# Attention and expert mixture on one core: loading the second batch's q and k behind all weights, in two-token runs, and turning them on TensorE

## The chip, the cores and the metric

The kernel runs on one core of one Trainium2 chip. The metric is the time of one execution on the device, in microseconds (us). Profiles are of one execution each; their time axis starts at the first instruction.

Engines: TensorE (PE; its weight loads are PEld), VectorE (DVE), ScalarE (ACT), GpSimd (POOL), SyncE (SP). DMAs of the loads that convert float32 to bf16 are issued from GpSimd, the plain stores and the DMA transposes from SyncE. Lines such as L679 are lines of the kernel's file; the changed kernel has other line numbers for the same statements, and both are named where it matters.

## The reference

Streaming attention with four sink tokens and a window of 128, then a dense mixture of four experts whose outputs are weighted by normalised probabilities:

```python
# q, k, v: (4 batches, 8 heads, 768 tokens, 64); all float32
scores = q @ k.T / 8, kept where key < 4 or 0 <= query - key < 128   # else -1e9
x = softmax(scores) @ v                      # (4, 768, 8 * 64) -> x: (3072, 512)
p = domain_probs / domain_probs.sum(-1)      # (3072, 4)
out = sum over e of p[:, e] * (relu(x @ w1[e]) @ w2[e])   # w1[e]: 512 x 1024, w2[e]: 1024 x 512
```

## The kernel before

The kernel is written as a list scheduler in Python: while it is being built it keeps a clock for each engine and for the DMA (the *issue clock*), and always emits next what should be ready first. The chip does not see this clock. What the clock decides is **the order of the instructions on each engine and in each DMA queue**, and an engine executes its instructions in that order. A wrong clock costs time only where it puts an instruction that is not ready in front of one that is.

Batch 0 goes through a plain mixture (a first layer, L679, and a second layer, L828). Batches 1 to 3 go through a seven-product form (L775), which needs sums of hidden blocks that VectorE makes (S0, S1, S2 and one in place). While batch b's mixture runs, batch b+1's attention is threaded in between.

How q and k get to have the head dimension on the partitions: batch 0's are loaded in runs of two tokens, regrouped on ScalarE or VectorE and transposed on TensorE. Those of the other batches are loaded token by token and turned by a DMA transpose that SyncE issues:

```python
def load_nat(b, tb):                       # one block of 128 tokens, q and k
    both = sb.tile([P, 2, H, D], BF16, name="qkn", tag="qkn", bufs=NQB)
    for i, src in enumerate((q, k)):
        nc.gpsimd.dma_start(out=both[:, i], in_=src[b, :, tb * P:(tb + 1) * P, :].rearrange("h p d -> p h d"))
    ...
    lands(("qk", b, tb), 3 * H * P * D * 4)

def turn_nat(b, tb):
    nc.sync.dma_start(out=qkT[b][..., tb * P:(tb + 1) * P]..., in_=nat[b, tb]..., transpose=True)
    turned_at[b, tb] = max(t["pe"], landed["qk", b, tb]) + TURN          # TURN = 3500 ns

def lands(key, nbytes):                    # the DMA's issue clock
    dma["at"] += nbytes / 350.0
    landed[key] = dma["at"] + 1500
...
        if not att.more() and not loaded:  # batch 0's attention is done: queue batch 1's loads
            nat_loads(1, range(2)); v_loads(1, 0); gates_by_row()
            nat_loads(1, range(2, NQB)); ...
            loads += [(load_w1, 3), (load_w2, 3)]        # the last expert's weights, last
            turns += [(1, tb) for tb in range(NQB)]
```

The sums, and a buffer that two things share: S2 has the tag `wide2`, and so has the output tile of batch 0's last pair of token blocks, which SyncE stores.

```python
                nc.vector.tensor_add(S[0][:, e], H21, H22)
                nc.vector.tensor_sub(H21, H11, H21)
                nc.vector.tensor_sub(S[1][:, e], S[0][:, e], H11)
...
                S[2] = mo.tile([P, E, QF, P], BF16, name="S2", tag="wide2", bufs=1)
                nc.vector.tensor_sub(S[2][:, e], H12, S[1][:, e])
# batch 0's outputs: out_sb[g] = mo.tile(..., name="osb0", tag=f"wide{g}", bufs=1)
                nc.sync.dma_start(out=out[r:r + P, :], in_=dst)
```

The hidden blocks (`hps`) go through four PSUM banks, which VectorE empties in batches 1 to 3 (L696). When VectorE stands still, TensorE can make four more and then has to stop.

The softmax here doesn't subtract the row's maximum and nothing guards it: scores larger than these inputs give would overflow.

## Time and profile before

| | |
|---|---|
| time, median (range) | 423.35 us (420.43 to 504.98, 3 runs; the 504.98 is a single outlier) |
| span of the profile | 420.6 us |
| TensorE busy | 379.2 us |
| VectorE busy | 257.1 us |
| mean granted TensorE clock | 0.955 |

Three rows of the page, part 2. Each digit is one of 40 equal slices (10.5 us each) in tenths: of the engine's busy share for PE, of the granted clock for PEclk, of the mean busy share of the DMA engines for DMA; 9 means 90% or more.

```profile
PE   5597891499999995999999999999999999999995
...
PEclk9589987599999996999999999999999999999999
DMA  9999999999423899131159911111301111010101
```

TensorE is nearly full from the 17th slice on. Before that it has two dents, the 1 and 4 in the seventh and eighth slices and the 5 in the sixteenth, and the clock's digits drop beside both (5 in the eighth, 6 in the sixteenth). The timeline of TensorE shows the first: start, duration, engine, line, operation, output<-inputs, shapes, count, and in brackets the idle time just before and what ended it.

```profile
78.94 0.51 PE L449 MATMUL sps<-qkT 64*128 64x256 bf16 x4 [13.83 <-DMA qkT<-qkn]
79.37 1.89 PE L679 MATMUL hps<-xT,w 128*128 128x256 bf16 x8
81.05 2.77 PE L828 MATMUL acc<-w,H 128*128 128x512 bf16 x8
```

The scores of batch 1 (L449) stand in front of the rest of batch 0's mixture and wait 13.83 us for the DMA transposes of q and k. The eight first-layer matmuls behind the wait take 1.68 us until the next start, where eight warm ones take 0.87. What else the DMA had to do at that time is in the issue order of GpSimd, whose lines are the loads (L131 q and k, L207 v, L219 and L224 weights):

```profile
55.89 4.42 POOL L207 DMA_DIRECT2D vx<-in_v_dram  x5
60.27 0.79 POOL L219 DMA_DIRECT2D w<-in_moe_w_dram  x1
61.26 0.89 POOL L224 DMA_DIRECT2D w<-in_moe_w_dram  x1 [0.20 <-issue]
```

The five v loads shown, twelve q/k loads ahead of them and one v load more, all in single-token runs, stand in front of the last expert's weights, which are issued at 60 us. The second hole, again from the timeline of TensorE, and beside it that of VectorE:

```profile
162.22 3.57 PE L679 MATMUL hps<-xT,w 128*128 128x256 bf16 x16 [5.11 <-DVE H L696]
165.59 0.54 PE L499 MATMUL od<-vx,aT 128*128 128x65 bf16 x6
```

```profile
161.15 0.42 DVE L741 TENSOR_TENSOR S<-H,S 128x512 bf16<-128x512 bf16 x1 [5.85 <-DMA out_dram<-osb]
161.49 0.68 DVE L696 SCALAR_TENSOR_TENSOR H<-hps,gates 128x512 bf16<-128x512 f32 x1
```

VectorE stands 5.85 us at S2 (L741), on the store whose buffer S2 reuses. The evictions of `hps` (L696) are behind it, and TensorE runs out of banks for 5.11 us. The sixteen matmuls behind the hole take 3.37 us until the next start, instead of 1.75. SyncE's queue at that time, in its order:

```profile
138.79 2.61 SPq L143 DMA_TRANSPOSE qkT<-qkn  x2
...
142.71 7.35 SPq L143 DMA_TRANSPOSE qkT<-qkn  x3
...
150.78 1.40 SPq L143 DMA_TRANSPOSE qkT<-qkn  x1
152.28 2.08 SPq L519 DMA_TRANSPOSE xT<-onat  x1
154.45 1.22 SPq L843 DMA_DIRECT2D out_dram<-osb  x2
```

### The profile page before, as it was taken

To read this page: it belongs to the slowest core of one execution; us is meant where nothing else is said; L and a number is where in the kernel's file an instruction comes from. 1 tells how busy PE (TensorE), PEld (TensorE's weight loads), DVE (VectorE), ACT (ScalarE), POOL (GpSimd) and SP (SyncE) were. 2 spreads that over 40 slices of the span, in tenths; PEclk is the share of its full clock that TensorE was granted. 3 is DMA by queue.
4 is the path that set the end of the run, shared out by engine and by line. 5 is a ranking of instruction groups with operands and counts; after the bars stand their busy time and mean duration, and the time that the engine had idled before them with its cause. 6 is when DMAs were issued, how large, how long until landed. Compare 5 with 4: busy or idle time off the path is not lost.

```text
span 420.6 us, 8232 instructions
## 1 busy us (share of the span) xinstructions
PE 379.2 (90%) x3530; PEld 299.5 (71%) x3530; DVE 257.1 (61%) x551; ACT 99.5 (24%) x161; POOL 70.3 (17%) x109
## 2 busy tenths in 40 slices
PE   5597891499999995999999999999999999999995
PEld 2365461266666663887888888788888888888884
DVE  3535551056645466957967967957749558485570
ACT  3556531154444421023111113221010000100000
POOL 8861281134010353000102000000000000000000
PEclk9589987599999996999999999999999999999999
DMA  9999999999423899131159911111301111010101
GB/s 170 191 194 210 184 155 155 140 115 213 30 26 51 145 194 151 51 37 51 53 51 119 197 25 51 52 27 51 77 0 51 51 51 50 2 51 2 50 2 50
DMA packets 108560, 37.10 MB, mean 88 GB/s; under 512 B 95988, under 2 KB 102228, under 8 KB 108524
## 3 DMA queue, kind: packets, MB, share of 16 engines
q0 software_dynamic: 72832, 17.31, 46.7%
q1 hardware_dynamic: 35692, 19.27, 21.8%
q8 instruction: 27, 0.44, 0.4%
q14 instruction: 9, 0.07, 0.1%
HBM read 40.45 MB, written 6.34 MB: 111 GB/s over the span
## 4 chain that ended last, share of the span: by engine, by line
PE 72%; DVE 11%; DMA 10%; ACT 3%; POOL 1%; issue 1%; DVEq 0%
PE hps L679 30%; PE acc L775 26%; PE acc L828 9%; DVE H L696 5%; DMA qkT<-qkn 4%; DMA qs<-in_k_dram 3%; PE sps L449 3%; PE od L499 2%; ACT aT L460 2%; DMA qkn<-in_q_dram 2%; DMA out_dram<-osb 1%; DVE S L727 1%; DVE S L741 1%; DVE aT L461 1%; DVE H L728 1%; DVE S L729 1%
## 5 line engine op out<-in xcount | busy, mean ns | idle before, releaser
L679 PE MATMUL hps<-xT,w 128*128 128x256 bf16 x1536 | 191.6, 278 | 7.4 <-DVE H L696 7.3
L679 PEld LDWEIGHTS <-w 128*128 128x128 bf16 x1536 | 149.0, 100 | 34.6 <-issue 13.0
L696 DVE SCALAR_TENSOR_TENSOR H<-hps,gates 128x512 bf16<-128x512 f32 x144 | 94.4, 685 | 23.5 <-PE hps L679 22.4
L460 ACT ACTIVATE aT<-sps 128x1024 bf16<-128x1024 f32 (+1 forms) x46 | 44.1, 959 | 84.9 <-PE sps L449 81.6
L775 PEld LDWEIGHTS <-H 128*128 128x128 bf16 x576 | 56.1, 98 | 7.3 <-issue 0.9
L461 DVE TENSOR_TENSOR aT<-aT,mask 128x1024 bf16<-128x1024 bf16 (+1 forms) x46 | 29.9, 649 | 39.7 <-ACT aT L460 39.6
L789 ACT COPY osb<-acc 128x256 f32<-128x256 f32 x36 | 13.4, 373 | 170.4 <-PE acc L775 166.7
L828 PE MATMUL acc<-w,H 128*128 128x512 bf16 x192 | 46.3, 385 | 0.0
L775 PEld LDWEIGHTS <-S 128*128 128x128 bf16 x432 | 41.9, 98 | 5.1 <-issue 0.3
L690 ACT ACTIVATE H<-hps 128x512 bf16<-128x512 f32 x48 | 28.7, 598 | 39.9 <-PE hps L679 39.9
L207 POOL DMA_DIRECT2D vx<-in_v_dram x24 | 21.3, 904 | 84.6 <-PE od L499 80.6
L775 PE MATMUL acc<-wf,H 128*128 128x256 bf16 x288 | 34.4, 273 | 0.5 <-ACT osb L789 0.5
L775 PE MATMUL acc<-w,S 128*128 128x256 bf16 x288 | 34.4, 273 | 0.0
L775 PE MATMUL acc<-w,H 128*128 128x256 bf16 x288 | 34.2, 273 | 0.0
L449 PE MATMUL sps<-qkT 64*128 64x128 bf16 (+1 forms) x256 | 18.6, 245 | 15.7 <-DMA qkT<-qkn 13.8
L828 PEld LDWEIGHTS <-H 128*128 128x128 bf16 x192 | 18.0, 99 | 19.0 <-issue 1.9
L449 PEld LDWEIGHTS <-qkT 64*128 64x128 bf16 x256 | 8.0, 94 | 25.6 <-issue 19.5
L131 POOL DMA_DIRECT2D qkn<-in_q_dram x18 | 15.8, 880 | 61.8 <-DMA qkT<-qkn 52.1
L838 DVE SCALAR_TENSOR_TENSOR osb<-acc,scale_t,osb 128x512 f32<-128x512 f32 x18 | 13.5, 751 | 17.3 <-PE acc L828 17.1
L499 PE MATMUL od<-vx,aT 128*128 128x65 bf16 x352 | 21.1, 198 | 2.9 <-DVE aT L461 2.9
L499 PEld LDWEIGHTS <-aT 128*128 128x128 bf16 x352 | 17.9, 101 | 5.7 <-DVE aT L461 4.0
L511 DVE TENSOR_TENSOR onat<-od,R 128x256 bf16<-128x256 f32 x48 | 20.4, 424 | 1.7
(77 smaller groups left out, 226.8 us busy)
## 6 DMA issues: line engine op xcount, KB each, us to landing
w<-in_moe_w_dram POOLq DMA_DIRECT2D x8, 1024.0 KB, 18.6
out_dram<-osb SPq DMA_DIRECT2D x24, 256.0 KB
gates<-gate_rows SPq DMA_DIRECT2D x9, 512.0 KB
vx<-in_v_dram POOLq DMA_DIRECT2D x24, 128.0 KB, 7.3
qkn<-in_q_dram POOLq DMA_DIRECT2D x18, 128.0 KB, 6.8
qkn<-in_k_dram POOLq DMA_DIRECT2D x18, 128.0 KB, 7.2
qraw<-in_q_dram SPq DMA_DIRECT2D x2, 256.0 KB
kraw<-in_k_dram SPq DMA_DIRECT2D x2, 256.0 KB
```

The costliest lines, as they stand in the source:

```text
L131: nc.gpsimd.dma_start(out=both[:, i], in_=src[b, :, tb * P:(tb + 1) * P, :].rearrange("h p d -> p h d"),)
L207: nc.gpsimd.dma_start(out=vx[tb][:, :, 0:D], in_=v[b, :, tb * P:(tb + 1) * P, :].rearrange("h p d -> p h d"),)
L449: nc.tensor.matmul(sps[ph][:, c:c + nq * P], lhsT=T[pr, 1, hp, kb * P:(kb + 1) * P], rhs=T[pr, 0, hp, qb * P:(qb + nq) * P], start=True, s ...
L460: nc.scalar.activation(out=a, in_=both[:, :, 0:w], func=AF.Exp, scale=scale)
L461: nc.vector.tensor_mul(a, a, m[:, None, :].to_broadcast([P, 2, w]))
L499: nc.tensor.matmul(od[:, qi, ph], lhsT=a[:, ph, c:c + P], rhs=vx[kb][:, 2 * hp + ph, 0:DX], start=(g == 0 and i == 0), stop=(i == len(term ...
L511: nc.vector.tensor_mul(o[:, :, hp].rearrange("p q (h d) -> p q h d", h=2), od[:, :, :, 0:D], R.to_broadcast([P, 2, 2, D]),)
L679: nc.tensor.matmul(h[:, i].rearrange("p (q n) -> p q n", q=2), lhsT=w1_sb[e][:, db, fb * P:(fb + 1) * P], rhs=xT[b, g][:, :, db], start=(i ...
L690: nc.scalar.activation(out=dst, in_=h, func=AF.Relu)
L696: nc.vector.scalar_tensor_tensor(out=dst, in0=h, scalar=0.0, in1=gate, op0=ALU.max, op1=ALU.mult,)
L775: nc.tensor.matmul(x, lhsT=self.operand(b, g, e, m)[:, f], rhs=forms[e][m][:, f], start=(i == 0 and m in ("P1", "P2", "P5")), stop=(i == n ...
L828: nc.tensor.matmul(op, lhsT=H[:, fb // QF, fb % QF, s], rhs=w2_sb[e][:, fb, :], start=(fb == 0), stop=(fb == NFB - 1),)
```

## The change

Its intent: take the first hole away by loading what batch 0's mixture still needs (the last expert's weights) ahead of batch 1, load batch 1's q and k in two-token runs and transpose them on TensorE as for batch 0, count DMA time by rows in the issue clock, and hold S2 back until the store should be done. The core of the diff:

```diff
-    PIECES = {b: [(0, 2), (G, 2), (2 * G, 2)] if b == 0 else [(0, NQB)] for b in range(B)}
+    PIECES = {b: [(0, 2), (G, 2), (2 * G, 2)] for b in range(2)}
...
-    def lands(key, nbytes):
-        dma["at"] += nbytes / 350.0
-        landed[key] = dma["at"] + 1500
+    ROW = {64: 31.0, 128: 40.0, 512: 97.0, 1024: 172.0}
+    def lands(key, rows, cols):
+        dma["at"] += rows * ROW[cols] / 16
+        landed[key] = dma["at"] + 2200
...   (load_qk: batch 1's pieces in tiles of their own, tag "qs", bufs=1)
+                if b == 1:
+                    self.todo += [("regroup", b, g, 0)] + [("transposes", b, g, hp) for hp in range(NHP)]
...
+                self.S_at[u] = t["dve"] + 60          # the other products no longer wait for S2
                 self.waiting.remove(u)
-                if busy((b, g), "P3"):
+                if busy((b, g), "P3") or t["dve"] < self.stored:
                     break
...
-                self.S_at[b, g, e] = dve(QF * P, rate=1.9, fixed=100)
+                self.S4_at[b, g, e] = dve(QF * P, rate=1.9, fixed=100)
...
                 nc.sync.dma_start(out=out[r:r + P, :], in_=dst)
+                self.stored = at + 4500
...
-            nat_loads(1, range(2))
-            v_loads(1, 0)
             gates_by_row()
-            nat_loads(1, range(2, NQB))
-            for g in range(1, NG):
-                v_loads(1, g)
             loads += [(load_w1, 3), (load_w2, 3)]
-            turns += [(1, tb) for tb in range(NQB)]
+            for g in range(NG):
+                loads += [(load_qk, 1, g), (load_v, 1, (2 * g,)), (load_v, 1, (2 * g + 1,))]
```

More of the change, by code (lines that the diff above doesn't have):

```diff
@@ L119, in load_qk @@
             both = mo.tile([P, 2, H, T * D], BF16, name="qs", tag="gates", bufs=2)
-            for i, src in enumerate((q, k)):
-                nc.gpsimd.dma_start(
-                    out=both[:, i], in_=src[b, :, s0:s0 + P * T, :].rearrange("h (p t) d -> p h (t d)", t=T),
-                )
-            nat[b, piece] = both
-            lands(("qk", b, piece), 2 * H * P * T * D * 4)
-            return
+        else:
+            both = sb.tile([P, 2, H, T * D], BF16, name="qs", tag="qs", bufs=1)
+        for i, src in enumerate((q, k)):
+            nc.gpsimd.dma_start(
+                out=both[:, i], in_=src[b, :, s0:s0 + P * T, :].rearrange("h (p t) d -> p h (t d)", t=T),
+            )
+        if b:
+            dma["at"] = max(dma["at"], pool(0, fixed=2400))
+        nat[b, piece] = both
+        lands(("qk", b, piece), 2 * H * P, T * D)
     def load_nat(b, tb):
@@ L136, in load_nat @@
         dma["at"] = max(dma["at"], at)
-        lands(("qk", b, tb), 3 * H * P * D * 4)
+        lands(("qk", b, tb), 2 * H * P, D)
     def turn_nat(b, tb):
@@ L160, in load_first @@
                 nat[0, half, name, "raw"] = x
-            lands(("first", half), 2 * 4 * P * T * D * 4)
+            lands(("first", half), 8 * P * 29 // 40, T * D)
     def copy(engine, out, in_):
@@ L212, in load_v @@
                 dma["at"] = max(dma["at"], pool(0, values_at[b - 1, min(NG - 1, (tb + 1) // 2)], fixed=1200))
-            lands(("v", b, tb), H * P * D * 4)
+            lands(("v", b, tb), H * P, D)
     w1_sb, w2_sb = {}, {}
@@ L219, in load_w1 @@
         nc.gpsimd.dma_start(out=w1_sb[e], in_=moe_w1[e].rearrange("(db p) f -> p db f", p=P))
-        lands(("w1", e), Dm * F * 4)
+        lands(("w1", e), Dm, F)
     def load_w2(e):
@@ L224, in load_w2 @@
         nc.gpsimd.dma_start(out=w2_sb[e], in_=moe_w2[e].rearrange("(fb p) d -> p fb d", p=P))
-        lands(("w2", e), Dm * F * 4)
+        lands(("w2", e), F, Dout)
     forms = {}
@@ L405, in sink_keys @@
             if b:
-                keys_at[b] = dve(8, turned_at[b, 0])
+                keys_at[b] = dve(8, *turned(b, 0))
     def sink_values(b):
@@ L416, in turned @@
     def turned(b, g, *hps):
-        if b == 0:
-            return [turned_at.get((0, g, hp), 1e12) for hp in hps or range(NHP)]
+        if b < 2:
+            return [turned_at.get((b, g, hp), 1e12) for hp in hps or range(NHP)]
         return [turned_at.get((b, tb), 1e12) for tb in range(2 * g + 2)]
@@ L554, in __init__ @@
             for g in groups:
+                if b == 1:
+                    self.todo += [("regroup", b, g, 0)] + [("transposes", b, g, hp) for hp in range(NHP)]
+                if b and g == 0:
+                    self.todo.append(("keys", b, 0, 0))
                 if b and g:
@@ L579, in options @@
                 elif kind == "keys":
-                    yield turned_at.get((b, 0), 1e12), "todo"
+                    yield max(turned(b, 0)), "todo"
                 elif kind == "sinks":
@@ L601, in emit @@
                     regroup(b, x)
+                    if (b, x) == (1, NG - 1):
+                        nat_loads(2, range(NQB))
+                        turns.extend((2, tb) for tb in range(NQB))
                 elif kind == "transposes":
@@ L643, in __init__ @@
             self.products = [(b, g, m) for b, g in PAIRS for m in CHAIN]
-            self.at = {}
-            self.done = 0.0
+            self.at, self.S4_at = {}, {}
+            self.done = self.stored = 0.0
         def more(self):
@@ L758, in product_ready @@
                 at = max(self.H_at[b, g, e] for e in range(E))
-            elif any((b, g, e) not in self.S_at for e in range(E)):
-                return 1e12
-            else:
-                at = max(self.S_at[b, g, e] for e in range(E))
+            else:
+                S_at = self.S4_at if m == "P3" else self.S_at
+                if any((b, g, e) not in S_at for e in range(E)):
+                    return 1e12
+                at = max(S_at[b, g, e] for e in range(E))
             return max(at - 1300, acc_free[m in ("P2", "P5", "P3")], max(forms_at.values()) if sum(formed.values()) == 4 * E else 1e12)
@@ L915 @@
             turn_nat(*x)
-            if x[1] == NQB - 1 and x[0] + 1 < B:
-                loaded += 1
-                nat_loads(loaded, range(NQB))
-                turns += [(loaded, tb) for tb in range(NQB)]
+            if x == (2, NQB - 1):
+                nat_loads(3, range(NQB))
+                turns += [(3, tb) for tb in range(NQB)]
         if ahead and t["dve"] < now + (3000 if len(used) == E else 300):
@@ L923 @@
                 weight_form(e)
-        if not att.more() and loaded > ahead and (not turns or turns[0] != (ahead + 1, 0)) and (ahead == 0 or mix.done >= sum(work[:ahead])):
+        if ahead + 1 < B and not att.more() and (ahead == 0 or (ahead + 1, 0) in turned_at) and (ahead == 0 or mix.done >= sum(work[:ahead])):
             ahead += 1
-            att = Attention(
-                ahead, [("keys", ahead, 0, 0)], range(NG),
-            )
+            att = Attention(ahead, [], range(NG))
             upto = mix.done
@@ L939 @@
         if min(o[0] for o in opts) > 1e11:
+            if mix.last and t["dve"] < mix.stored:
+                t["dve"] = mix.stored
+                mix.sums()
+                continue
             e = next((e for e in range(E) if form_due(e)), None)
```

## The prediction

> **What bounds the kernel now.** TensorE: 379.2 us busy of a 420.6 us span on the page, 72% of the chain of waits; VectorE is busy 61%. From 172 us to the end (windows) it is busy 240.4 of 249 us. Its timeline shows two real holes:
> 1. 65.1 to 78.94 us: 13.83 us, released by "DMA qkT<-qkn". The first scores of batch 1 stand in TensorE's order ahead of the rest of batch 0's mixture and wait for the DMA transpose of q/k. In the chain: a 6.4 us q load at 54.2 us, then 18.3 us of DMA transposes (60.6 to 78.9), which share the DMA engines with loads in 128-byte packets and the last expert's weights, issued at 60.3 us.
> 2. 157.1 to 162.22 us: 5.11 us. VectorE stands at the fourth sum (S2), 5.9 us on the "out_dram<-osb" store whose buffer S2 reuses; evictions of hps queue behind it and TensorE runs out of banks.
>
> Slow matmuls follow each hole: at 79.4 us eight first-layer matmuls take 1.68 us instead of 0.87, the next second-layer block 2.71 instead of 1.73; at 162.2 us sixteen take 3.37 instead of 1.75, the next eight 1.78. That is 2.0 and 2.8 us more. The Trainium skill, "TensorE: Matmul & The Clock Gate", Part 1, says an idle array falls back to half rate until it has been busy again; the granted clock agrees (0.65 and 0.70 in those stretches, 1.00 between).
>
> **What the change does.**
> - Removes hole 1: the last expert's weights are issued right behind the others (weights landed every 5 us, so at about 50 to 60 us), batch 1's q/k follow in two-token pieces, and its scores move behind some 17 us more of batch 0's mixture. The first piece should land near 65 us; its transposes stand at about 81 us. Gain 13.8 + 2.0.
> - Removes hole 2: S2 is held back in issue order until the store should be done, and the other products no longer wait for it. Gain 5.1 + 2.8.
> - Adds to TensorE 48 transposes in groups of four, 0.23 us a group as in batch 0: 2.8 us, all on the path.
> - Adds to ScalarE/VectorE 6 regroupings and 12 copies of 0.6 to 0.7 us each, some 12 us, where both are half idle: free.
> - Takes away six DMA transposes and halves the rows of batch 1's q/k.
> - New risk: batch 2's transposes can start only when batch 1's last scores are done; TensorE now has about 4.8 us of work between these (before: 12.9). One transpose took about 3.7 us from issue to release, two about 5: I allow 1.5 us of wait. The early order also holds the first second-layer block back: 1 us.
>
> Sum: -15.8 - 7.9 + 2.8 + 2.5 = -18.4 us. From 420.4 to 423.4 us: **403.5 us**, range 399 to 410. Faster by over 2%: 0.95; within 2%: 0.04; slower: 0.01.
>
> **What would show it.** No TensorE wait on qkT<-qkn over 1 us at 60 to 80 us; no wait of S2 on out_dram; granted clock near 1.00 from 60 us on; the first piece landed over 10 us before its transposes; the part after batch 2's first scores unchanged in length.
>
> **What would make it wrong.** Pieces landing later than placed, so that a regrouping stops evictions; a wait of several us, plus slow matmuls, at batch 2's first scores, where VectorE also stands at the sink keys in front of evictions; S2 still waiting on the store.

## The result

The changed kernel takes 406.64 us (404.69 to 407.25, 4 runs) against 422.38 us of the kernel before in the same count (4 runs). The ratio is 0.963 (95% interval 0.958 to 0.969). Ratios here are the mean time of one kernel's fast runs over that of the other's of the same rounds, so they are not quite the ratios of the medians quoted. Executions over 1.5% slower than the fastest of the same kernel are left out of the means.

The same rows of the changed kernel's page (slices of 10.1 us):

```profile
PE   6588979999999998999999999999999999999995
...
PEclk9998869999999999999999999999999999999999
DMA  9999995063994999926269111111411011010101
```

Both dents are gone: from the seventh slice to the last but one TensorE has 9s and one 8, and the clock has nothing under 9. The DMA row shows a 0 in the eighth slice where it had a 9.

The loads, in GpSimd's timeline (L223 and L228 are the weights, L124 is q and k):

```profile
26.82 0.75 POOL L223 DMA_DIRECT2D w<-in_moe_w_dram  x1 [0.51 <-DMA qs<-in_q_dram]
28.58 0.89 POOL L228 DMA_DIRECT2D w<-in_moe_w_dram  x1 [1.01 <-DMA qs<-in_k_dram]
29.46 0.88 POOL L124 DMA_DIRECT2D qs<-in_q_dram  x1
...
85.62 0.87 POOL L124 DMA_DIRECT2D qs<-in_q_dram  x1 [44.47 <-DVE H L703]
```

The last expert's weights are issued at 26.8 and 28.6 us instead of 60 us, and batch 1's first piece right behind. Nothing of q/k is issued from then until 85.6 us. The table of windows (columns: stretch, its length, busy us and count of each engine, granted clock, DMA share, GB/s) shows when that piece had landed:

```profile
core 0: us, PE busy (x) PEld busy (x) DVE busy (x) ACT busy (x) POOL busy (x), PEclk, DMA share, GB/s
64.00:65.00 1.00, 1.00 (x6) 0.46 (x5) 0.00 (x0) 0.43 (x1) 0.00 (x0) 1.00 0.04 11
65.00:85.00 20.00, 19.89 (x140) 13.73 (x141) 10.65 (x17) 7.17 (x12) 0.00 (x0) 1.00 0.00 1
```

By 65 us the DMA engines are idle, 21 us before TensorE's first transposes of it (L392) in the timeline:

```profile
86.20 0.39 PE L392 MATMUL tr<-ident,qkn 128*128 128x128 bf16 x4
86.42 1.04 PE L690 MATMUL hps<-xT,w 128*128 128x256 bf16 x8
...
92.50 0.34 PE L453 MATMUL sps<-qkT 64*128 64x256 bf16 x4
```

Groups of four transposes are followed by the next work 0.22 us later, so the twelve groups cost 2.6 to 2.7 us of TensorE's time. The second hole is gone too. In VectorE's timeline S2 stands later, at 151.98 us, and has no bracket, that is no wait:

```profile
151.98 0.75 DVE L753 TENSOR_TENSOR S<-H,S 128x512 bf16<-128x512 bf16 x2
```

SyncE's queue now has the stores ahead of the transposes:

```profile
130.19 12.44 SPq L856 DMA_DIRECT2D out_dram<-osb  x4
142.85 5.88 SPq L147 DMA_TRANSPOSE qkT<-qkn  x4
```

At batch 2's first scores, where the prediction feared a wait, there is a small one:

```profile
147.59 0.34 PE L453 MATMUL sps<-qkT 64*128 64x256 bf16 x4 [0.59 <-DMA qkT<-qkn]
```

What is worse than before is the start. TensorE's timeline of the kernel before, then of the changed one, up to the first block of forty first-layer matmuls, which is the first instruction after batch 0's attention:

```profile
28.03 1.90 PE L828 MATMUL acc<-w,H 128*128 128x512 bf16 x8
...
53.52 5.51 PE L679 MATMUL hps<-xT,w 128*128 128x256 bf16 x40
```

```profile
28.22 0.40 PE L453 MATMUL sps<-qkT 64*128 64x128 bf16 x6 [1.27 <-ACT aT L464]
...
30.02 3.10 PE L841 MATMUL acc<-w,H 128*128 128x512 bf16 x7
...
38.44 0.30 PE L503 MATMUL od<-vx,aT 128*128 128x65 bf16 x4 [1.32 <-DVE aT L465]
...
57.33 6.46 PE L690 MATMUL hps<-xT,w 128*128 128x256 bf16 x40
```

The block starts 3.8 us later. In the new order two groups of scores and the first values stand in front of the first second-layer block, which starts at 30.02 us instead of 28.03, and TensorE waits for ScalarE and VectorE (1.27 and 1.32 us; the largest such wait in the kernel before is 0.98 us after 20 us).

Where the 15.0 us between the two profiles went, by two marks that both have (the block of forty, and the first of the seven-product matmuls at 173.74 and 161.05 us): the start costs 3.8 us, the stretch between the marks is 16.5 us shorter (120.2 to 103.7), and the rest is 2.3 us shorter, of which 0.9 us is a first-layer group of eight that now stands before the mark (the other 1.4 us I have not traced).

### The profile page after: what moved, and what is told of

The parts are those of the page before. It is cut to its first block, busy times and chain, and to the rows that moved or that the text cites. A ratio compares the mean times of both kernels' runs of the same rounds, so it can differ in the third digit from the quotient of the medians.

```text
span 405.6 us, 8310 instructions
## 1 busy us (share of the span) xinstructions
PE 382.3 (94%) x3566; PEld 304.4 (75%) x3578; DVE 262.0 (65%) x562; ACT 104.8 (26%) x168; POOL 65.2 (16%) x103
## 4 chain that ended last, share of the span: by engine, by line
PE 77%; DVE 14%; DMA 3%; ACT 3%; issue 1%; POOL 1%; DVEq 0%; ACTq 0%
PE hps L690 32%; PE acc L788 27%; PE acc L841 11%; DVE H L707 6%; DMA qs<-in_k_dram 3%; PE sps L453 3%; PE od L503 2%; ACT aT L464 2%; DVE aT L465 2%; PE tr L392 1%; DVE S L738 1%; DVE S L753 1%; DVE H L739 1%; DVE S L740 1%; DVE onat L515 1%
## 5 line engine op out<-in xcount | busy, mean ns | idle before, releaser
L841 PE MATMUL acc<-w,H 128*128 128x512 bf16 x180 | 44.8, 387 | 0.7 <-issue 0.2
L701 ACT ACTIVATE H<-hps 128x512 bf16<-128x512 f32 x46 | 27.4, 597 | 29.4 <-PE hps L690 29.4
L738 DVE TENSOR_TENSOR S<-H 128x512 bf16<-128x512 bf16 x36 | 15.3, 425 | 8.8 <-PE acc L788 7.8
L788 PE MATMUL acc<-wf,S 128*128 128x256 bf16 x144 | 17.2, 273 | 0.0
```

What stands on the lines that cost most here:

```text
L701: nc.scalar.activation(out=dst, in_=h, func=AF.Relu)
L788: nc.tensor.matmul(x, lhsT=self.operand(b, g, e, m)[:, f], rhs=forms[e][m][:, f], start=(i == 0 and m in ("P1", "P2", "P5")), stop=(i == n ...
L841: nc.tensor.matmul(op, lhsT=H[:, fb // QF, fb % QF, s], rhs=w2_sb[e][:, fb, :], start=(fb == 0), stop=(fb == NFB - 1),)
```

## The experiments

Twelve runs, all correct. "Block" is the start of the block of forty matmuls in the profile.

| run | what it is | median us | ratio to before (95%) | block at | span |
|---|---|---|---|---|---|
| again | changed kernel | 406.36 | 0.963 (0.958 to 0.967) | 55.99 | 403.9 |
| early_bytes | changed, early loads counted by bytes | 408.67 | 0.968 (0.964 to 0.972) | 53.72 | 406.7 |
| measured_rows | changed, row times from the trace | 414.05 | 0.980 (0.976 to 0.985) | 53.20 | 410.8 |
| dma_turns | changed, batch 1 by DMA transposes | 405.99 | 0.961 (0.956 to 0.965) | 57.21 | 406.3 |
| hold_alone | before + hold of S2 (4.5 us) | 421.17 | 0.999 (0.991 to 1.007) | 54.98 | 421.8 |
| hold20_alone | before + hold of S2 (20 us) | 414.77 | 0.990 (0.982 to 0.997) | 53.73 | 413.3 |
| weights_first | before + weights first | 412.19 | 0.980 (0.974 to 0.986) | 52.62 | 408.7 |
| weights_first_act_stores | the same, stores from ScalarE's queue | 407.30 | 0.974 (0.967 to 0.981) | 54.49 | 405.3 |
| no_hold | changed without the hold | 407.03 | 0.967 (0.962 to 0.972) | 55.98 | 404.2 |
| rows_long_hold | measured_rows + hold of 20 us | 402.53 | 0.956 (0.951 to 0.961) | 54.41 | 401.4 |
| weights_first_hold20 | before + weights first + hold of 20 us | 399.25 | 0.955 (0.949 to 0.961) | 52.81 | 398.1 |
| dma_rows_hold | dma_turns + measured rows + hold of 20 us | 402.18 | 0.962 (0.955 to 0.969) | 54.76 | 400.3 |

Four kernels ran together in each of three sets: (again to dma_turns), (hold_alone, weights_first, no_hold, rows_long_hold), and the other four. The kernel before itself scatters from 414.6 to 428.7 us over the three sets, so a ratio depends on which of its runs count as fast: in the third set one run of 414.57 us narrowed that choice, and 399.25 over its median of 421.71 would be 0.947 where the ratio says 0.955. I therefore compare versions by their medians as well.

### Set 1: the start, and who removed the first hole

**again** is the yardstick, the changed kernel unaltered.

> The changed kernel once more, as the yardstick of this set of runs. Expected: ratio to the kernel before about 0.963, span 403 to 406 us, with TensorE's first block of forty matmuls after batch 0's attention starting near 57.3 us (53.5 in the kernel before). If the late start is luck of the clock and not the order, it should differ here by more than a microsecond from the first profile.

It repeats the first result (406.36 us). The block starts at 55.99 us, 1.3 us earlier than in the first profile, so there is some luck in that number, but it is still later than in any kernel with the old early order (table).

**early_bytes** takes only the early part of the new clock away:

```diff
+    dma["bytes"] = 2500.0
+
     def lands(key, rows, cols):
         dma["at"] += rows * ROW[cols] / 16
         landed[key] = dma["at"] + 2200
+        if key[0] == "first" or key[1] == 0 or key[0] in ("w1", "w2") and key[1] < 3:
+            dma["bytes"] += (2 * 4 * P * 2 * D * 4 if key[0] == "first" else rows * cols * 4) / 350.0
+            landed[key] = dma["bytes"] + 1500
```

> The changed kernel with the issue clock counting batch 0's loads and the first three experts' weights by bytes again, so that TensorE's order up to the end of batch 0's attention is that of the kernel before. Theory (the row clock places the first expert's second weights at 33 us, they land at 25, so the order puts scores and values that wait for ScalarE and VectorE in front of the first second-layer block, and the idle time slows the clock): the block of forty starts at 53.5 to 54.5 us, and the kernel is 3 to 4.5 us faster than the changed one, less up to 2 us because the scores of batch 2 now stand only about 3 us behind the last scores of batch 1. Rival (the early loss is the clock's chance state): the block starts at 55 to 58 us as in the changed kernel, no gain.

The block moved to 53.72 us as the theory said, but the time did not fall: 408.67 us. The new order has only some 3 us of work between batch 1's last scores and batch 2's first ones, and TensorE's timeline shows what that costs:

```profile
147.62 0.34 PE L458 MATMUL sps<-qkT 64*128 64x256 bf16 x4 [2.25 <-DMA qkT<-qkn]
...
150.12 0.50 PE L458 MATMUL sps<-qkT 64*128 64x256 bf16 x4 [0.90 <-ACT aT L469]
150.55 9.07 PE L695 MATMUL hps<-xT,w 128*128 128x256 bf16 x56
```

Two waits of 2.25 and 0.90 us, and behind them 56 first-layer matmuls that take 8.90 us until the next start (159.45 us), where warm ones take 6.1 (seven groups of 0.87). So the gain at the start was spent again here.

**measured_rows** sets the issue clock's row times from the trace instead of those that the change was written with:

```diff
-    ROW = {64: 31.0, 128: 40.0, 512: 97.0, 1024: 172.0}
+    ROW = {64: 14.0, 128: 25.0, 512: 82.0, 1024: 150.0}
```

> The changed kernel with the row times of the issue clock set from the trace (14, 25, 82 and 150 ns instead of 31, 40, 97 and 172). Theory: early order as in the kernel before, block of forty at 53.5 to 54.5 us; batch 1's first transposes stand at about 65 us, where the first piece has landed at about 62; 8 us of work stand in front of batch 2's scores, so no wait there. Span 399 to 401 us, ratio 0.950 to 0.955, the fastest of this set. Rival (the changed kernel needs its 20 us of slack behind the pieces): a wait of several us on the pieces at 60 to 70 us and no gain.

The early order and the block are as expected (53.20 us), the pieces caused no wait at 65 us, and yet it is 7.7 us slower than the changed kernel. Its timelines of SyncE, VectorE and TensorE say why:

```profile
144.07 0.53 SPq L856 DMA_DIRECT2D out_dram<-osb  x1
144.70 3.87 SPq L147 DMA_TRANSPOSE qkT<-qkn  x1
148.67 0.53 SPq L856 DMA_DIRECT2D out_dram<-osb  x1
```

```profile
155.50 0.76 DVE L753 TENSOR_TENSOR S<-H,S 128x512 bf16<-128x512 bf16 x2 [9.42 <-DMA out_dram<-osb]
```

```profile
156.87 7.37 PE L690 MATMUL hps<-xT,w 128*128 128x256 bf16 x48 [8.70 <-DVE onat L515]
```

The second hole is back, larger: S2 waits 9.42 us and TensorE 8.70. The last store of batch 0 is issued at 148.67 us, behind a DMA transpose, although VectorE had finished its data at 138.3 us. The hold of 4.5 us that the change has was there all the same. This is the run that put the hold in question, and the order in SyncE's queue in its place.

**dma_turns** undoes the two-token runs and TensorE's transposes for batch 1 and leaves everything else of the change:

```diff
-    PIECES = {b: ... for b in range(2)}
+    PIECES = {b: ... for b in range(1)}
...
-                loads += [(load_qk, 1, g), (load_v, 1, (2 * g,)), (load_v, 1, (2 * g + 1,))]
+                loads += [(load_nat, 1, 2 * g), (load_nat, 1, 2 * g + 1), (load_v, 1, (2 * g,)), (load_v, 1, (2 * g + 1,))]
+            turns += [(1, tb) for tb in range(NQB)]
```

> The changed kernel with batch 1's q and k loaded in single-token runs and turned by DMA transposes as before, still behind all weights and with the row clock. Theory (the order of the loads and the place of batch 1's scores removed the first hole, not TensorE's transposes): no hole over 1 us at 65 to 100 us, and as the 48 transposes (2.8 us) are gone, 1.5 to 3 us faster than the changed kernel. Rival (TensorE's transposes are what removed the hole, as DMA transposes are slow beside loads): a wait of over 3 us on the transposes, slower than the changed kernel by 2 us or more.

No wait on a transpose at batch 1's first scores at 91.45 us. So TensorE's transposes did not remove the first hole; loads and scores in another place did. The time equals that of the changed kernel (405.99 against 406.36 us), not the 1.5 to 3 us less that was expected: here S2 waits 2.27 us on the store once more, TensorE stops for 0.90 and 1.55 us, and 48 matmuls behind it take 7.07 us until the next start instead of 5.2.

### Set 2: the two parts alone

**hold_alone** puts only the hold of S2 into the kernel before (the `stored`, `S_at` and `S4_at` lines of the diff above).

> The kernel before with the hold of S2 alone (S2 is issued only when the last store of batch 0 should be done by the issue clock, and the other products no longer wait for it). Theory of the prediction (the hold removes the second hole, 5.1 us and 2.8 us of slow matmuls behind it): 6 to 9 us faster than the kernel before, ratio about 0.981, no wait of S2 on the store over 1 us. Rival (how long the store takes is set by the DMA transposes that stand in front of it in the same queue, and 4.5 us of hold is too little for that): S2 still waits 3 us or more and the gain is under 4 us. The first hole stays at about 14 us in both.

The ratio is 0.999, a gain of at most 0.9%. In its profile S2 still waits 1.6 us and TensorE stops for 0.90 and 0.86 us with slow matmuls behind. From the end of the first hole to the end of the kernel it takes 338.0 us (421.8 - 83.83) against 341.7 in the kernel before (420.6 - 78.94): some 3.7 us of the 7.9 that I had expected. The whole span shows nothing of it because the first hole ended 4.9 us later in this execution, with the same instructions up to there. When the DMA transposes that run beside the loads end differs from one execution to the next: 78.94, 83.83 and, in hold20_alone, 78.37 us.

**weights_first** moves two lines of the kernel before and nothing else:

```diff
+            gates_by_row()
+            loads += [(load_w1, 3), (load_w2, 3)]
             nat_loads(1, range(2))
             v_loads(1, 0)
-            gates_by_row()
             nat_loads(1, range(2, NQB))
             for g in range(1, NG):
                 v_loads(1, g)
-            loads += [(load_w1, 3), (load_w2, 3)]
             turns += [(1, tb) for tb in range(NQB)]
```

> The kernel before with the last expert's weights issued ahead of batch 1's loads, and nothing else: single-token runs, DMA transposes and the byte clock stay. Theory (order of the loads and the place of batch 1's scores made the first hole): the wait on the transposes falls from 13.8 to under 5 us, 9 to 15 us faster than the kernel before, ratio 0.965 to 0.98. Rival (the DMA transposes beside single-token loads are too slow whatever the order): a wait of over 8 us at 75 to 95 us, gain under 5 us.

The first hole is gone entirely; no wait of TensorE on a DMA transpose is left in the whole trace. Batch 1's first scores:

```profile
75.52 0.34 PE L449 MATMUL sps<-qkT 64*128 64x256 bf16 x4
```

As the loads' landing times drive the issue clock, this order also moves batch 1's scores back behind more of batch 0's mixture: TensorE comes to them at 75.5 us, where it came to them at 65.1 in the kernel before. So of the 13.8 us some 10.4 are the later place, and the transposes had to end only 3.4 us earlier than before (by 75.5 instead of 78.94 us). That they did end earlier shows in SyncE's queue too: each of batch 1's six DMA transposes holds the queue for 4.33 us in the median and 10.26 at most in the kernel before, for 2.55 and 3.57 here. The two effects were not tested apart. The gain is smaller than the hole, because the second one has doubled (view of waits: engine and line, releaser, total us, times, longest):

```profile
DVE S L741 <- DMA out_dram<-osb: 10.8, 1, 10.8
PE hps L679 <- DVE H L696: 13.6, 7, 11.0
```

VectorE had the last output of batch 0 at 134.2 us; SyncE issued its store at 143.1 us, behind transposes, and S2 was released at 149.8 us.

**no_hold** takes the hold out of the changed kernel; TensorE's order stays.

```diff
-                if busy((b, g), "P3") or t["dve"] < self.stored:
+                if busy((b, g), "P3"):
...
-                S_at = self.S4_at if m == "P3" else self.S_at
+                S_at = self.S4_at
-            if mix.last and t["dve"] < mix.stored:
+            if False:
```

> The changed kernel without the hold of S2: TensorE's order is the same, S2 is issued with the other sums. Theory of the prediction (the hold removed the second hole): S2 waits on the store, TensorE runs out of banks, 5 to 8 us slower than the changed kernel. Rival (in the changed kernel the stores stand in front of batch 2's transposes in their queue and are done at about 146 us, so the hold has little left to do): a wait of 1 to 3 us on VectorE that the four banks mostly cover, 0 to 3 us slower.

Nothing changes: 407.03 us. The timeline of VectorE has S2 at the place where the sums are, without a bracket, that is without a wait:

```profile
144.97 0.42 DVE L753 TENSOR_TENSOR S<-H,S 128x512 bf16<-128x512 bf16 x1
```

The hold in the changed kernel does put S2 later (151.98 us), but the time does not need it. What removed the second hole there, as the order in the traces has it, is that batch 1's attention ends later relative to batch 0's mixture, so the four last stores of batch 0 stand ahead of batch 2's transposes in SyncE's queue (shown above, 130.19 before 142.85 us). That this place matters is tested below (weights_first_act_stores).

**rows_long_hold** is measured_rows with `self.stored = at + 20000`.

> The kernel with row times set from the trace (measured_rows), and the hold of S2 lengthened from 4.5 to 20 us. Theory (measured_rows won its 4 us at the start, and lost them where S2 stood 9.4 us on a store that sat behind a DMA transpose in the queue: an 8.7 us hole and 2 us of slow matmuls): the hole is gone, span 399 to 401 us, ratio 0.947 to 0.954, faster than the changed kernel by 1 to 1.5%. Rival (the hole at 148 us came from batch 1's work standing too close to batch 2's): a hole of over 5 us stays there.

The hole of 8.7 us is gone, the early order kept, and it is 4.5 us faster than no_hold in the same set and 3.8 us faster than again. Between the profiles of no_hold and this run (404.2 and 401.4 us) 1.6 of 2.8 us are the start of the block; most of the rest should be the waits of 0.6 and 0.9 us at batch 2's first scores in no_hold, which are absent here.

### Set 3: what the best combination is, and the store

**weights_first_hold20** joins the two-line move with the hold, lengthened; no two-token runs, no TensorE transposes, byte clock.

> The kernel before with the last expert's weights ahead of batch 1's loads and a hold of S2 of 20 us; batch 1 stays with single-token runs and DMA transposes. Theory (load order removes the first hole, and the second is S2 on a store that stands behind DMA transposes in its queue, so a hold long enough removes it too, and TensorE's transposes only cost 2.8 us): no TensorE wait over 1 us after 60 us, span 394 to 398 us, ratio 0.936 to 0.945, faster than the changed kernel by 2% and than rows_long_hold by 1%. Rival (turning on TensorE is worth something of its own): not faster than 401 us.

399.25 us, the fastest of all, 7 us under the changed kernel (406.36 and 406.64 us, other sets) and 3.3 us under rows_long_hold (402.53). The span is 398.1 us, at the upper edge of what was expected. Both holes are gone; the largest stop of TensorE on an eviction is 0.8 us:

```profile
PE hps L679 <- DVE H L696: 2.8, 7, 0.8
```

It is faster than rows_long_hold by about what 48 transposes cost (2.7 us), but that does not show that they are the reason: 1.6 us of the difference is the start of the block (52.81 against 54.41 us), and dma_rows_hold below, which is rows_long_hold without TensorE's transposes, takes 402.18 us against 402.53.

**hold20_alone** is the kernel before with the long hold only.

> The kernel before with the hold of S2 at 20 us, and nothing else. Theory: S2 no longer waits on the store (5.9 us before, 1.6 us with 4.5 us of hold) and TensorE has no stop over 1 us at 155 to 170 us; measured from the end of the first hole, 7 to 8 us faster than the kernel before; whole ratio 0.978 to 0.987 if the first hole is not longer than before. Rival (the second hole only moves): the stretch from batch 1's first scores to the end is shorter by less than 4 us, as with the short hold.

No wait of S2 and no stop of TensorE over 1 us at that place. From the end of the first hole to the end it takes 334.9 us (413.3 - 78.37): 6.8 us less than the kernel before, against 3.7 us for the short hold. So the second hole was worth about 7 us of the 7.9 that were costed, but it takes a hold of the length of the queue's delay to get it.

**weights_first_act_stores** leaves S2 where it was and changes the queue of the six stores:

```diff
-                nc.sync.dma_start(out=out[r:r + P, :], in_=dst)
+                nc.scalar.dma_start(out=out[r:r + P, :], in_=dst)
```

> weights_first with batch 0's six stores issued from ScalarE's queue instead of the queue of the DMA transposes, and no hold at all. Theory (S2 waits 10.8 us because the store is issued late, behind DMA transposes that wait for their loads in the same queue): the store is done within 4 us of its sum, S2 waits under 2 us, the 11 us hole is gone, span 395 to 399 us, ratio 0.936 to 0.947. Rival (the store is slow because the DMA engines are busy): S2 still waits over 5 us.

Half right. The wait falls from 10.8 to 3.7 us and TensorE's hole from 11.0 to 4.0:

```profile
DVE S L741 <- DMA out_dram<-osb: 3.7, 1, 3.7
PE hps L679 <- DVE H L696: 6.6, 7, 4.0
```

The store is now issued at about 138.2 us, as soon as its data are there, but S2 is released only at 146.3 us. So about 7 of the 11 us were the place behind the transposes in the queue. From its issue to the release of S2 the store then takes some 8 us while earlier DMA transposes and loads are under way; in no_hold, where batch 2's transposes are issued only behind it, it was done within 3.9 us (last store issued by 141.1, S2 at 145.0 without a wait). Whether the transposes or the loads make it slow I have not separated.

**dma_rows_hold** tried to find where DMA transposes are too slow: batch 1's scores stand at 73 us, close behind its single-token loads.

> weights_first_hold20 in the changed kernel's frame, with the row times set from the trace: batch 1's first scores stand at about 73 us, some 6 us earlier, while its single-token loads are still in flight. Theory (DMA transposes do as well as TensorE's as long as the scores stand late enough; beside loads they are slow, four took 18 us in the kernel before): a wait of 3 to 10 us on the transposes at 73 to 85 us, span 399 to 406. Rival (only the weights in front mattered): no wait over 1 us, span 394 to 398.

```profile
73.41 0.34 PE L453 MATMUL sps<-qkT 64*128 64x256 bf16 x4 [0.85 <-DMA qkT<-qkn]
```

The wait is only 0.85 us, so my theory of slow DMA transposes beside loads is not borne out here: with the weights out of the way they end at 73.4 us, 5 us before the earliest end with the weights behind (78.37). The wait is what the rival said; the span (400.3 us) is in the range of the theory, not of the rival. It is 2.2 us longer than that of weights_first_hold20, and the block starts 2.0 us later in it (54.76 against 52.81). This difference is no scatter of single executions (398.8 to 401.3 us there, 402.0 to 403.5 here); why two kernels with the old early order start so differently was not found.

This run and rows_long_hold differ only in who transposes batch 1's q and k, as dma_turns and again do. Both pairs are equal within 0.4 us (402.18 and 402.53; 405.99 and 406.36). So doing without the 48 transposes frees 2.7 us of TensorE, but no pair of runs shows a gain in time of that size; in dma_rows_hold the wait of 0.85 us and in dma_turns the stops at S2 took part of it back.

## Why the prediction was right, and where not

The time (403.5 us, range 399 to 410) and the direction were right. Point by point:

1. **The first hole** (gain 13.8 + 2.0): right, and for the reason given. The weights first and the scores later removed it (weights_first, dma_turns). (The clock of 0.65 in the prediction is that of the hole itself; over the slow matmuls behind it, 78.94 to 84 us, it is 0.62.) The piece landed by 65 us, as predicted, and its transposes stand at 86 us instead of 81. The prediction left open what the two-token runs and TensorE's transposes were needed for, and no run here shows a use for them: dma_turns has no first hole without them.
2. **The second hole** (gain 5.1 + 2.8): it went, but the step "S2 is held back in issue order until the store should be done" is not what removed it; that the hole went all the same was luck. Without the hold the changed kernel is as fast (no_hold), and with the hold alone the kernel before gains only some 3.7 us behind the first hole (hold_alone). By the order of the queues the hole went because the stores moved ahead of the DMA transposes in SyncE's queue, a side effect of batch 1's attention being later. Where that order tips over, the hole returns in spite of the hold (measured_rows, 8.7 us). The size was nearly right: hold20_alone got 6.8 us of 7.9 back.
3. **TensorE's transposes** (2.8 us): 2.6 to 2.7 us by the pitch of 0.22 us a group. Regrouping and copies caused no stop of TensorE over 1 us at 65 to 145 us, as predicted.
4. **Batch 2's first scores** (allowed 1.5 us): 0.59 us, then small stops of 0.23, 0.90 and 0.51 us, in which scores share one PSUM bank pair. About 2.2 us together. The prediction also named the part behind these scores as unchanged in length; it is 258.0 us (405.6 - 147.59) against 269.0 (420.6 - 151.65), some 3 us shorter even without the 7.9 of the second hole.
5. **The early order** (allowed 1 us): this is the term of the sum that was mis-sized. The block of forty starts at 56.0 to 57.3 us in the four profiles with the change's row times (mean 56.6) and at 52.6 to 55.0 us in the ten profiles with the old early order (mean 53.8): about 2.8 us. The row clock puts the landing of the first expert's second weights at 33 us; in the kernel before the first block that uses them starts at 28.03 us without waiting for them, and they had landed by 25.4 us, if I read GpSimd's waits rightly: its load at 25.45 us waits for a weights DMA, each of its next loads that waits on a DMA fits the one eight places before it, and eight places before this one are the weights in question. So the order puts waiting work in front of ready work. The block of forty itself took 6.46 us instead of 5.51, but that is not the order's doing: it took 6.1 to 6.5 us in ten of the twelve profiles of the experiments, with the old early order too.

For the stretch between the marks: -23.7 (both holes with what follows them) + 2.7 (transposes) + 0.9 (a group of eight more) + 1.0 (block of forty, which was short in the profile of the kernel before) + 2.2 (stops at batch 2's scores) = -16.9, measured -16.5.

Three things stay open: how much of the late start is the order and how much the chance state of the clock in a given execution (it scatters by 1.4 us in one group and 2.4 in the other); what exactly makes the end of the DMA transposes vary by 5 us in the kernel before; and what slows a store that is issued behind transposes.

## What to carry to other kernels

When two holes vanish with one change, undo each part by itself before crediting it: here the two-line move of the loads and a hold of sufficient length give more (399.25 us) than the change (406.6 us), whose new transposes brought nothing that a run shows and whose new row times cost time (402.53 us with others and a long hold). A DMA queue is an order like any engine's: before asking how long a store takes, look at what stands in front of it, and hold back a buffer's next use for that long, or give the buffer to something else. An issue clock that is too pessimistic costs time too, where it puts waiting work ahead of ready work; compare its landing times with the trace.

## What the Trainium skill lacked or had wrong

- "DMA: Bandwidth & Descriptors", Issuing engines are not separate DMA queues, says that issuing from several engines saves only the sequencer's time to initiate a DMA, usually small beside the DMA itself. Here the issuing engine's queue held a store back for 8.9 us (weights_first: data at 134.2, issued at 143.1 us, behind DMA transposes, the last of which alone took 3.52 us of the queue); issuing from ScalarE cut the wait from 10.8 to 3.7 us. This section does not speak of the wait behind earlier DMAs of the same issuing engine.
- The same page has no figure for a plain store issued while DMA transposes are in flight: 6.5 us (weights_first) and about 8 us (weights_first_act_stores) from issue to release for 256 KB behind or beside them, against at most 3.9 us ahead of them (no_hold).
- "TensorE: Matmul & The Clock Gate", Part 1, gives about 3.4 us of idle time until the clock falls back. It also says that frequent short idles between groups of matmuls make the clock go back and forth, but without a length. In early_bytes waits of 2.25 and 0.90 us, 2.5 us apart, were followed by 56 matmuls in 8.90 us instead of 6.1 (granted clock 0.72 from 147.6 to 160 us), in dma_turns waits of 0.90 and 1.55 us by 48 in 7.07 instead of 5.2. So gaps shorter than 3.4 us, close together, were followed by slow matmuls.
- "TensorE: Matmul & The Clock Gate", Part 4, gives about 275 ns for a transpose in a kernel. As a latency the trace has 219 ns in the median (changed kernel, 96 transposes), less than the page's, and what it takes from TensorE's time here is 0.22 us for four.
